# Four layers of linear and memory attention: where VectorE's weight maxima, idle TensorE time, cleared keys and the reading product are put

## The chip, the cores and the metric

The kernel runs on one core of one Trainium2 chip. The metric is the device time of one execution in microseconds (us); a time given without more is the median of several runs. The engines are called TensorE (PE in the profile, its weight loads PEld), VectorE (DVE), ScalarE (ACT), GpSimd (POOL) and SyncE (SP, which here only issues DMAs). On chip a tensor lies in SBUF or, as the output of TensorE, in one of eight PSUM banks.

## The reference

The input has 2048 rows of 640 columns: 32 heads of 20. Layers A, B, A, B follow each other, each added to its input:

```python
x = x + A(layernorm(x)); x = x + B(layernorm(x))     # twice, with the same weights

def A(x, wqkv, wo):                                  # linear attention
    q, k, v = split(x @ wqkv)                        # per head
    phi = lambda t: where(t > 0, t + 1, exp(t)) + 1e-6
    kv, z = einsum("hsd,hse->hde", phi(k), v), sum_s(phi(k))
    return ((phi(q) @ kv) / (phi(q) @ z + 1e-6)) @ wo

def B(x, wq, wk, wv, wo, beta):                      # 4 segments of 512 rows
    for each segment:
        a_dot = softmax(q k^T / sqrt(20) + causal) v
        a_mem = (phi(q) M) / (phi(q) z + 1e-6)       # memory of the segments before
        o = sigmoid(beta) a_mem + (1 - sigmoid(beta)) a_dot
        M, z = M + phi(k)^T v, z + sum(phi(k))
    return o @ wo
```

## The kernel before

**Streams and queues.** Two Python generators, one for the dense work and one for attention, are stepped in turn by their planned costs; a generator may be woven with an auxiliary one, which is advanced `per` steps after each step of the main one. A `pause(n)` is n empty steps. So the order in which instructions are *traced* is written by hand, and on TensorE that order is the order of its queue (`MANUAL = ("PE",)`). The queues of the other engines are put in order at compile time by a list scheduler with a model of durations: an instruction that is ready early in that model may stand ahead of others that were traced before it. `issue_after(ins)` keeps the instructions of a block that run on the engine of `ins` behind `ins`. Each queue is worked off in order.

**Precision.** Most products are made of three f16 products: each f32 operand is split in an upper f16 half (written by ScalarE) and a lower one (written by VectorE). Weights are scaled by a power of two first, and for that `w_prep` (L228 to L274) loads a weight into a `stage` buffer (two of them), takes five maxima over 640 columns on VectorE (L240) and one over these (L245), turns it on TensorE (L249), takes the maximum of the row (L251), spreads it with a product of one column (L255), makes scale and inverse (L258 to L261), and writes the ten halves (L266, L267). The pauses between these steps are `wait` auxiliary steps.

**The opening (`opening`, L1108 to L1192)** is layer A's first half on the input: four segments of four row tiles. A row tile is normed (`moments`, `normed`), turned by five identity products (`turn`, L321) and split. The key weights A k come first. `g_first` makes per segment the keys (`keys`: two halves of 320 columns, 15 products each at L397; `phi_a` on ScalarE and VectorE, L409 to L412; the lower half at L534, which is kept as `self.keyed`), the queries (`queries`, stored to DRAM as `pqd`), and adds to the memory the products of keys and normed input (`memory`, ten groups of 12 products, L571; taken up by VectorE at L591 or L593). The other weights are prepared as auxiliary steps: A q in segment 0, A v and A o in segment 1, B v and B q in 2, B k, B o and the gates (`gates`, L196 to L212) in 3. There the auxiliary generator goes two steps for one.

**The merge (`merge`)** ends the last segment: the sum of keys is spread over all rows (L636) and inverted (L638), the memory is scaled and split (`ge`, L652 to L655), multiplied by the value weights (L669), masked to the heads (L677) and written as two f16 halves into a row tile `kt` with zeros around (L674 to L681), and multiplied by the output weights (L702, L708; split into `wm` at L711, L712).

**Reading (`p_read`, L729 to L743)**: a row tile of stored queries is loaded (`p_load`, L726), multiplied by the spread key sum `zb` (L735), summed per head (L738), inverted (L739, L740) and multiplied by the inverse (L741). Then `a_second` turns it, multiplies it by `wm` (L397), adds the residual, and norms it for layer B. `a_head` reads the first three row tiles of a segment, `a_second` the fourth. In segment 0 the three are loaded by `a_head`, in the later ones within `p_read`.

**Layer B** projects a segment (`b_project`) while attention runs on the one before: the row maxima (L966, and L972 on VectorE), their split (L981, L982) and turn (L990), the scores and their exponentials (L1007, L1011), the causal selection on GpSimd (L1018) and the weighted sum (L1034). All row-shaped buffers share one pool of 11 (`ROWS`).

Of the kernel before, what the change touches and what calls it, by code (L numbers as in the profile page):

```python
# [10 lines left out]
F16 = mybir.dt.float16  # L11
# [116 lines left out]
def pause(n):  # L128
    for _ in range(n):
        yield 0.0  # L130
# [12 lines left out]
class Kernel:  # L143
# [84 lines left out]
    def w_prep(self, key, stage, w, wait=0, behind=None):  # L228
# [23 lines left out]
        yield 100.0  # L252
        yield from pause(wait)
        pb = self.bank()
# [56 lines left out]

    def turn(self, src, dst, i):
# [302 lines left out]
    def merge(self, L, wv, wo, memory, fill):  # L617
# [24 lines left out]
        for n in range(2):  # L642
# [4 lines left out]
            for c in range(C):  # L647
# [7 lines left out]
                nc.vector.tensor_tensor(t[:, c, 1, :HN], e, t[:, c, 0, :HN], op=OP.subtract)  # L655
        L["zb"] = zb
        for _ in memory:
            pass
        yield from filled(1)
        kt = []  # L660
        for t in range(C):
            p = self.bank()
            lo, hi = LO[t] * DH, (HI[t] + 1) * DH
            first = True
            for n in range(2):
                a, b = max(lo, n * HN), min(hi, (n + 1) * HN)
                for c in range(C if a < b else 0):
                    for k, m in ((0, 0), (0, 1), (1, 0)):
# [3 lines left out]
                        first = False  # L672
            k2 = sb.tile([P, 2, SEG], F16, tag="row", name="kt", bufs=ROWS)
            nc.vector.memset(k2, 0.0)  # L674
            e = sb.tile([P, 512], F32, tag="er", name="ke", bufs=3)[:, :hi - lo]
# [5 lines left out]
            L["split"] = nc.vector.tensor_tensor(k2[:, 1, P:P + hi - lo], e, k2[:, 0, P:P + hi - lo], op=OP.subtract)  # L681
            kt.append(k2)
            yield 15 * (hi - lo) * COL
# [45 lines left out]
    def p_read(self, L, s, i, o, pq=None):  # L729

        nc = self.nc
        if pq is None:
            pq = self.p_load(L, s, i)
        with self.tc.issue_after(L["split"].ins):
            nc.gpsimd.tensor_tensor(pq, pq, L["zb"][:, :D], op=OP.mult)  # L735
        q3 = pq.rearrange("p (h e) -> p h e", e=DH)
        rc = self.sb.tile([P, H], F32, tag="rca", name="rca", bufs=3)
        nc.vector.tensor_reduce(rc, q3, axis=AX.X, op=OP.add)  # L738
        nc.vector.tensor_scalar(rc, rc, 1e-6, 1 / P_ONE, op0=OP.add, op1=OP.mult)  # L739
        nc.vector.reciprocal(rc, rc)  # L740
        nc.gpsimd.tensor_tensor(q3, q3, rc[:, :, None].to_broadcast([P, H, DH]), op=OP.mult)  # L741
        o.append(pq)
        yield 0.0  # L743


    def a_head(self, L, s, box):

        while L["zb"] is None:
            yield 0.0
        box.update(o=[], oT=[])  # L750
        pq = [None] * 3
        if L["kt"] is None:
            pq = [self.p_load(L, s, i) for i in range(3)]
        while L["kt"] is None:
            yield 0.0
        box["oT"].append(self.new_oT())
        for i in range(3):
# [350 lines left out]
    def opening(self, src, stage, L, box):  # L1108
# [3 lines left out]
        def prep(key, keep=True):  # L1112
            w = self.w_tile(key) if keep else stage.tile([P, C, 2, D], F16, tag="split", name="split", bufs=1)
            if keep:
                self.w[key] = w
            yield from self.w_prep(key, stage, w, 0 if key[0] == "A" and keep else 6 if key == ("B", "o") else 3,
                                   {("A", "q"): self.lower, ("A", "v"): self.keyed}.get(key))

# [19 lines left out]

        self.lower = self.keyed = None
        cur = [None, self.x_t(), self.xs_t(0)]  # L1140
# [5 lines left out]
        x += [self.load_x(src, 0, i) for i in range(1, NT)]  # L1146
        first = self.normed(*m)
        yield from self.turn(first, cur[1], 0)
        with self.tc.high_priority():
            for _ in range(4):  # L1150
                next(k)
            with self.tc.issue_after(self.last.ins):
                m = self.moments(x[1])
            with self.tc.issue_after(self.taken.ins):
                w("k")
# [20 lines left out]
        for s in range(NSEG):  # L1176
            nxt = []
            if s == 0:
                q = a("q")
                n = self.norms(src, 1, nxt, 6)  # L1180
                aux = chain(o, islice(q, 3), pause(8), islice(q, 1), pause(2), islice(n, 1), pause(4), q, n)
            elif s == 1:
                aux = chain(self.norms(src, 2, nxt, 6), a("v"), a("o"), late())
            elif s == 2:
# [147 lines left out]
```

## Time and profile before

| | |
|---|---|
| median of 3 runs | 1723.12 us (1722.1 to 1726.43) |
| the profiled execution | 1722.49 us, span 1720.7 us |
| mean granted TensorE clock | 0.995 |
| TensorE busy | 1643.5 us (96%) |
| VectorE busy | 1244.5 us (72%) |
| ScalarE busy | 993.7 us (58%) |
| GpSimd busy | 535.6 us (31%) |
| HBM read, written | 109.32 MB, 78.64 MB |

How to read the lines that follow. A line of a timeline gives the start from the span's begin, the duration, engine, source line, operation, output<-inputs, and how many were merged into it; in square brackets, how long the engine sat idle before and what released it. A line of stretches gives the window, its length, and per engine the busy time with the number of instructions in brackets, in the order PE, PEld, DVE, ACT, POOL, then the granted clock of TensorE, the share of the DMA engines' time and GB/s. A line of waits gives who waited for whom, the sum in us, how often, and the longest. A line of groups gives the sum and the mean in ns of one, then the idle time before them and its causes. "SPq" is the time in which SyncE issues a DMA, not the transfer.

### The profile page before, as it was taken

How to read it: one execution, taken by the hardware profiler on the slowest of the kernel's cores; microseconds unless marked ns; L12 is line 12 of the kernel's file. 1: busy time of each engine (PE TensorE's matmuls, PEld its weight loads, DVE VectorE, ACT ScalarE, POOL GpSimd, SP SyncE). 2: the span in 40 equal slices, each digit the busy share in tenths (PEclk: the TensorE clock that was granted, in tenths of full speed). 3: DMA queues.
4: the chain of work that ended last, by engine and by line, in shares of the span. 5: the costliest groups of instructions: out<-in, count | busy, mean ns of one | idle time of the engine just before them, and what ended most of it. 6: DMA issues, size and time to landing. Idle time of an engine off the chain costs nothing.

```text
span 1720.7 us, 36268 instructions
## 1 busy us (share of the span) xinstructions
PE 1643.5 (96%) x13032; PEld 1031.4 (60%) x13032; DVE 1244.5 (72%) x3951; ACT 993.7 (58%) x1888; POOL 535.6 (31%) x1050
## 2 busy tenths in 40 slices
PE   6989989999999999999999999999999999999998
PEld 4767756554465566556556777766446545645555
DVE  7788886397787678759874466837787777878773
ACT  5666533346656646667775554433675575666673
POOL 3432224032223332334352311221431432233452
PEclk9999999999999999999999999999999999999999
DMA  6424654422222331453211303523132323223432
GB/s 216 154 86 151 225 205 142 138 93 73 95 78 69 109 121 55 126 178 97 75 52 44 110 31 123 196 92 124 64 106 77 112 82 109 93 84 111 145 104 93
DMA packets 110365, 190.89 MB, mean 111 GB/s; under 512 B 14172, under 2 KB 69596, under 8 KB 107624
## 3 DMA queue, kind: packets, MB, share of 16 engines
q1 hardware_dynamic: 97704, 142.68, 25.6%
q0 software_dynamic: 3264, 24.91, 4.0%
q10 hardware_dynamic: 9216, 20.98, 3.1%
q8 instruction: 103, 1.69, 0.4%
q14 instruction: 78, 0.64, 0.1%
HBM read 109.32 MB, written 78.64 MB: 109 GB/s over the span
## 4 chain that ended last, share of the span: by engine, by line
PE 71%; DVE 14%; ACT 7%; issue 3%; DMA 3%; POOL 2%; SPq 0%; ACTq 0%; POOLq 0%; DVEq 0%
PE ps L397 29%; PE ps L383 13%; PE ps L1034 7%; PE ps L571 5%; PE ps L1007 4%; PE ps L966 3%; PE ps L321 3%; ACT pe L1011 3%; DVE ps L972 2%; PE ps L448 2%; PE ps L851 2%; PE ps L1047 1%; DVE wmx L240 1%; DVE e L412 1%; DVE split L267 1%
## 5 line engine op out<-in xcount | busy, mean ns | idle before, releaser
L972 DVE CUSTOM_DVE_ANT_0 ps<-ps,maskw 128x384 f32<-128x384 f32 (+3 forms) x1024 | 473.1, 519 | 39.3 <-PE ps L966 36.6
L1011 ACT ACTIVATE pe<-ps,lsc 128x512 f32<-128x512 f32 x640 | 395.8, 697 | 76.2 <-PE ps L1007 74.8
L397 PEld LDWEIGHTS <-xT 128*128 128x128 f16 x2880 | 281.5, 98 | 115.5 <-issue 6.3
L1018 POOL TENSOR_SCALAR_AFFINE_SELECT pe<-pe 128x256 f32<-128x256 f32 (+1 forms) x640 | 229.6, 366 | 369.4 <-ACT pe L1011 362.8
L397 PEld LDWEIGHTS <-oT 128*128 128x128 f16 x1920 | 185.6, 98 | 82.1 <-issue 5.9
L1034 PE MATMUL ps<-pe,v 128*32 128x512 f32 (+3 forms) x2048 | 164.3, 436 | 12.5 <-POOL pe L1018 7.3
L397 PE MATMUL ps<-w_Ak,xT 128*128 128x320 f16 x960 | 142.8, 306 | 3.2 <-ACT w_Ak L266 1.2
L972 DVE DVE_READ_ACCUMULATOR2_ANT mg<- 128x1 f32 x1024 | 144.4, 141 | 0.0
L397 PE MATMUL ps<-wm,oT 128*128 128x320 f16 x960 | 141.0, 300 | 3.2 <-DVE oT L326 2.3
L397 PE MATMUL ps<-w_Bo,oT 128*128 128x320 f16 x960 | 142.4, 301 | 1.8 <-ACT oT L325 1.1
L383 PE MATMUL ps<-xT,w_Bq 128*128 128x512 f16 x600 | 140.3, 380 | 2.8 <-ACT r L421 1.6
L397 PE MATMUL ps<-w_Bv,xT 128*128 128x320 f16 x960 | 139.7, 300 | 1.2 <-DVE otok L1054 1.2
L571 PE MATMUL ps<-pk,xs 128*128 128x321 f16 (+1 forms) x960 | 139.4, 303 | 0.9 <-DVE pk L534 0.5
L383 PE MATMUL ps<-xT,w_Bk 128*128 128x512 f16 x600 | 138.4, 380 | 1.2 <-ACT pe L1011 1.2
L397 PE MATMUL ps<-w_Aq,xT 128*128 128x320 f16 x960 | 137.9, 300 | 0.1
L966 PE MATMUL ps<-ks,qs 60*128 60x512 f16 (+3 forms) x1024 | 123.2, 298 | 6.7 <-ACT pe L1011 3.2
L571 PEld LDWEIGHTS <-xs 128*128 128x128 f16 x960 | 93.7, 98 | 39.6 <-issue 2.1
L816 DVE SCALAR_TENSOR_TENSOR nat<-ps,nat 128x512 f16<-128x512 f32 x80 | 55.1, 689 | 82.6 <-ACT nat L815 82.4
L1034 PEld LDWEIGHTS ps<-pe,v 128*32 128x32 f32 x2048 | 65.4, 109 | 74.4 <-issue 39.3
L412 DVE SCALAR_TENSOR_TENSOR e<-e,r 128x320 f32<-128x320 f32 x128 | 68.2, 533 | 56.5 <-ACT r L411 56.2
L1007 PE MATMUL ps<-qs,ks 62*128 62x512 f16 (+3 forms) x1024 | 106.5, 300 | 2.2 <-ACT pe L1011 1.1
L815 ACT ACTIVATE nat<-ps 128x512 f16<-128x512 f32 x80 | 48.3, 603 | 88.5 <-PE ps L383 72.3
(197 smaller groups left out, 2395.9 us busy)
## 6 DMA issues: line engine op xcount, KB each, us to landing
x<-xn ACTq DMA_DIRECT2D x48, 320.0 KB
qs<-qd SPq DMA_DIRECT2D x128, 120.0 KB
ks<-kd SPq DMA_DIRECT2D x128, 120.0 KB
xo<-x SPq DMA_DIRECT2D x48, 320.0 KB
pqi<-pqd SPq DMA_DIRECT2D x32, 320.0 KB
qd<-nat SPq DMA_DIRECT2D x40, 256.0 KB
kd<-nat SPq DMA_DIRECT2D x40, 256.0 KB
x<-in_A_x SPq DMA_DIRECT2D x16, 320.0 KB
```

Of the source, the lines that this page charges most:

```text
L321: nc.tensor.transpose(pt[:, (c - c0) * P:(c - c0 + 1) * P], src[:, c * P:(c + 1) * P], self.ident)
L383: nc.tensor.matmul(p, w[:, c, a, t * P:(t + 1) * P], xT[:, c, b, :], start=k == 0, stop=k == 3 * C - 1)
L397: nc.tensor.matmul(p, xT[:, c, a, i * P:(i + 1) * P], w[:, c, b, n * HN:(n + 1) * HN], start=k == 0, stop=k == 3 * C - 1)
L412: nc.vector.scalar_tensor_tensor(e, e, 1.0, r, op0=OP.min, op1=OP.add)
L571: nc.tensor.matmul(p, xs[:, i, a, c * P:(c + 1) * P], pk[i][:, b, cols], start=i == 0 and a == b, stop=i == NT - 1 and a == 1)
L816: nc.vector.scalar_tensor_tensor(nat[:, 1], p, QK_SHIFT, nat[:, 0], op0=OP.mult, op1=OP.subtract)
L966: nc.tensor.matmul(bs[par][:, a:a + n], qs[r, p, i * P:(i + 1) * P], ks[r, p, :n], start=True, stop=True)
L972: nc.vector.tensor_tensor_reduce(bs[par][:, a:a + n], bs[par][:, a:a + n], self.maskw[:, SEG - n:], 1.0, NEG, OP.add, OP.max, G["mg"][:, p ...
L1007: nc.tensor.matmul(b[:, a:a + n], ks[r, p, j * P:(j + 1) * P], qs[r, p, j * P:], start=True, stop=True)
L1011: nc.scalar.activation(e, b, AF.Exp, scale=self.lsc)
L1018: nc.gpsimd.affine_select(d, d, pattern=pat, compare_op=OP.is_ge, fill=0.0, base=0, channel_multiplier=-1)
L1034: nc.tensor.matmul(G["pv"][32 * h4:32 * h4 + 32, j * P:], v[j][:, h * E1:h * E1 + 32], G.pop((p, par, j)), start=j == 0, stop=j == 2, skip ...
```

## The change

- `w_prep`: for the output weight of B the pause between the maximum's turn and its spreading is 12 auxiliary steps instead of 6.
- `opening`: the five maxima of A v are kept behind the last key step of segment 0 (`self.first`) instead of the one that was traced last when the preparation begins, in segment 1.
- `busy(n)`: n products of the f32 identity with itself (128x128) into a bank that nobody reads; 10 before the first turn, 5 after it, 3 behind the preparation of the key weights' scale.
- `merge`: the five `kt` tiles are taken together ahead of the products, and GpSimd clears the two stretches of each that are read as zeros and not written, where VectorE cleared the whole tile.
- `merge`, `a_head`: the three loads of segment 0 are traced in the merge, ahead of the remaining memory products (`L["pre"]`).
- `p_read`: the product with `zb` stays on GpSimd for these three tiles and goes to VectorE for the 13 others of each of the two layers A. There the bound of `issue_after` (behind the last `kt` half) holds, since both are on VectorE.

```diff
 w_prep
-        yield from pause(wait)
+        yield from pause(2 * wait if key == ("B", "o") else wait)
         pb = self.bank()
         nc.tensor.matmul(pb[:, :1], self.ones, m2, start=True, stop=True)
...
+    def busy(self, n):
+        p = self.bank()
+        for _ in range(n):
+            self.nc.tensor.matmul(p[:, :P], self.ident, self.ident, start=True, stop=True)
...
 merge
         L["zb"] = zb
+        L["pre"] = [self.p_load(L, 0, i) for i in range(3)]
         for _ in memory:
             pass
         yield from filled(1)
-        kt = []
-        for t in range(C):
+        kt = [sb.tile([P, 2, SEG], F16, tag="row", name="kt", bufs=ROWS) for _ in range(C)]
+        for t, k2 in enumerate(kt):
+            nc.gpsimd.memset(k2[:, :, 64:P], 0.0)
+            nc.gpsimd.memset(k2[:, :, P + (HI[t] + 1 - LO[t]) * DH:320], 0.0)
+        for t, k2 in enumerate(kt):
             p = self.bank()
...
-            k2 = sb.tile([P, 2, SEG], F16, tag="row", name="kt", bufs=ROWS)
-            nc.vector.memset(k2, 0.0)
...
-            kt.append(k2)
...
 p_read
+        eng = nc.gpsimd
         if pq is None:
-            pq = self.p_load(L, s, i)
+            pq, eng = self.p_load(L, s, i), nc.vector
         with self.tc.issue_after(L["split"].ins):
-            nc.gpsimd.tensor_tensor(pq, pq, L["zb"][:, :D], op=OP.mult)
+            eng.tensor_tensor(pq, pq, L["zb"][:, :D], op=OP.mult)
...
 a_head
-        while L["zb"] is None:
-            yield 0.0
         box.update(o=[], oT=[])
-        pq = [None] * 3
-        if L["kt"] is None:
-            pq = [self.p_load(L, s, i) for i in range(3)]
         while L["kt"] is None:
             yield 0.0
+        pq = L["pre"] if s == 0 else [None] * 3
...
 opening
-                                   {("A", "q"): self.lower, ("A", "v"): self.keyed}.get(key))
+                                   {("A", "q"): self.lower, ("A", "v"): self.first}.get(key))
...
-        self.lower = self.keyed = None
+        self.lower = self.keyed = self.first = None
...
         first = self.normed(*m)
+        self.busy(10)
         yield from self.turn(first, cur[1], 0)
+        self.busy(5)
         with self.tc.high_priority():
             for _ in range(4):
                 next(k)
+            self.busy(3)
...
             elif s == 1:
+                self.first = self.keyed
                 aux = chain(self.norms(src, 2, nxt, 6), a("v"), a("o"), late())
```

## The prediction

> **What bounds the kernel now.** I read the page's busy shares first (its first line), then the stretches of ten microseconds, then TensorE's waits, and last the timelines of the places that the change touches.
>
> ```profile
> PE 1643.5 (96%) x13032; PEld 1031.4 (60%) x13032; DVE 1244.5 (72%) x3951; ACT 993.7 (58%) x1888; POOL 535.6 (31%) x1050
> ```
> ```profile
> 100.00:110.00 10.00, 5.30 (x35) 3.48 (x34) 9.46 (x15) 7.89 (x16) 6.76 (x9) 0.80 0.00 1
> 220.00:230.00 10.00, 5.08 (x38) 3.41 (x35) 5.00 (x10) 0.21 (x1) 1.66 (x2) 0.95 0.63 234
> 230.00:240.00 10.00, 8.68 (x48) 5.71 (x49) 10.00 (x25) 5.66 (x10) 3.52 (x3) 0.71 0.01 2
> 240.00:250.00 10.00, 9.16 (x104) 7.26 (x102) 9.80 (x22) 3.42 (x8) 0.92 (x3) 1.00 0.51 183
> ```
> ```profile
> PE ps L1034 <- POOL pe L1018: 7.3, 12, 1.2
> PE ps L255 <- DVE wm L251: 6.6, 2, 6.2
> PE ps L249 <- DVE wm L245: 6.5, 2, 4.7
> ...
> PE pm L990 <- DVE m L982: 2.9, 2, 1.5
> ```
>
> TensorE is busy for 96% of a span of 1720.7 us, so 77 us of idle time are all that any wait removed can return (span less 1643.5), and its order is written by hand: a microsecond saved at one place arrives at the end unless a later wait takes it. Two waits stand out: 4.7 us on a transpose of weight maxima (L249) and 6.2 us on the broadcast of one (L255). The stretches show where: 100 to 110 and 220 to 240, and there the granted clock falls to 0.80 and 0.71, so each wait is also paid in slow products behind it.
>
> **The opening (identity products).**
>
> ```profile
> 7.83 1.33 PE L321 MATMUL ps<-ident,xh 128*128 128x128 f32 x5 [7.83 <-ACT xh L370]
> ...
> 15.67 6.14 PE L397 MATMUL ps<-w_Ak,xT 128*128 128x320 f16 x26 [0.17 <-DVE w_Ak L267]
> ...
> 58.78 16.46 PE L397 MATMUL ps<-w_Aq,xT 128*128 128x320 f16 x120
> ```
> ```profile
> 2.73 0.23 DVE L167 CAST ident<-ident 128x128 f16<-128x128 f32 x1 [1.38 <-DMA ident<-in_const]
> ...
> 15.08 4.24 DVE L267 SCALAR_TENSOR_TENSOR w_Ak<-stage,scl_Ak,w_Ak 128x320 f16<-128x320 f32 x9
> ```
> ```profile
> 12.86 4.63 ACT L266 ACTIVATE w_Ak<-stage,scl_Ak 128x320 f16<-128x320 f32 x10 [3.28 <-DMA stage<-in_A_wqkv]
> 18.80 0.53 ACT L409 ACTIVATE e<-ps,inv_Ak 128x320 f32<-128x320 f32 x1 [1.31 <-PE ps L397]
> ...
> 21.85 0.53 ACT L409 ACTIVATE e<-ps,inv_Ak 128x320 f32<-128x320 f32 x1 [0.67 <-PE ps L397]
> ```
>
> The first 26 projection products take 6.14 us, 0.236 each; later the same form takes 16.46/120 = 0.137. So they run largely at the slow rate, although the stretch's clock column does not say so. The identity is there at 2.73 and the first turn starts at 7.83: 5.1 us in which ten products fit. A product of two f32 operands of this size is not in the trace; a transpose of the same size takes 1.33/5 = 0.27 slow. It is bounded by that 0.27 and by its double, 0.54; I take the middle, 0.40, since only one row bears on it. Ten then end at 6.7, before the turn; at 0.54 they end at 8.1 and delay it by 0.3. The five and the three others lie under the round trip of the maxima and add 0.5 at worst, as the upper bound has it. If the array is warm at 13.5, the products are held by VectorE's lower halves (end 19.32) rather than by the array: the first half can end at 17.5, when ScalarE's ten copies end (12.86 + 4.63), not 18.80, and the second near 19.9 (19.3 and the queue on ScalarE), not 21.85. ScalarE and VectorE carry the chain from there to 43 us, so I take **-1.9** (bounds -2.3 and +0.8).
>
> **The maxima of the values' weights (`self.first`).**
>
> ```profile
> 27.07 2.94 SPq L236 DMA_DIRECT2D stage<-in_A_wqkv  x5
> ```
> ```profile
> 42.34 0.72 DVE L534 SCALAR_TENSOR_TENSOR pk<-e,k_scl,pk 128x320 f16<-128x320 f32 x1 [0.64 <-ACT pk L547]
> ```
> ```profile
> L240 DVE TENSOR_REDUCE wmx<-stage 128x1 f32<-128x640 f32 x40 | 31.4, 807 | 1.7 <-DMA stage<-in_B_wk 1.0 <-DMA stage<-in_B_wo 0.7
> ```
> ```profile
> 108.61 0.37 PE L249 MATMUL ps<-ident,wm 128*1 128x128 f32 x1 [4.70 <-DVE wm L245]
> 108.78 4.21 PE L397 MATMUL ps<-w_Ak,xT 128*128 128x320 f16 x15
> ...
> 117.31 11.65 PE L571 MATMUL ps<-pk,xs 128*128 128x321 f16 x84
> ```
>
> The five reductions (5 x 0.807 = 4.0 us) are bound behind a key step of segment 1 and so stand in a VectorE queue that is 9.46 of 10 busy, while TensorE waits 4.70. Bound behind the last key step of segment 0 (42.34) they may go as soon as their data, issued at 27.07, is there: far earlier. In front of them stands segment 0's key step, behind them the residuals of the query weights; those feed the 120 products at 58.78, whose 16.46 us cover the rest, so I cost the move at nothing (4.0 if all five fell ahead of the query weights). The gain: 4.70 of wait, and 4.21 - 15 x 0.137 = 2.15 of slow clock, 6.85 in all. What is late next is the last pair of keys on VectorE, which has 4.0 us less to do and the other weight's five reductions (L240 again) still between. The products at 117.31 could start at 110.5; I let 0.85 of it be lost, one reduction's length: **-6.0** (bounds -6.9 and -2.9).
>
> **The output weight's pause, and the merged keys.**
>
> ```profile
> 231.32 0.58 PE L255 MATMUL ps<-wm,ones 1*128 1x1 f32 x2 [6.24 <-DVE wm L251]
> ...
> 249.88 2.45 PE L669 MATMUL ps<-xT,w_Av 128*128 128x80 f16 x35 [0.65 <-DVE xT L655]
> ...
> 264.98 1.94 PE L397 MATMUL ps<-wm,oT 128*128 128x320 f16 x13 [1.57 <-DVE oT L326]
> ```
> ```profile
> 225.29 0.17 DVE L211 TENSOR_SCALAR cg<-cg 128x8 f32<-128x8 f32 x1 [4.96 <-ACT cg L209]
> ...
> 231.05 0.22 DVE L251 TENSOR_REDUCE wm<-ps 1x1 f32<-1x128 f32 x1
> ```
> ```profile
> L674 DVE MEMSET kt<- 128x512 uint32 x10 | 4.8, 485 | 0.5
> L194 POOL MEMSET v<- 128x32 f32 x16 | 2.1, 167 | 21.9 <-DVE ge L652 21.9
> ```
> ```profile
> 1101.67 1.94 PE L397 MATMUL ps<-wm,oT 128*128 128x320 f16 x13 [0.71 <-DVE oT L326]
> ```
>
> Two auxiliary steps follow each step of segment 3, so six more pauses put L255 behind three more memory products, 3 x 12 x 0.137 = 4.9 us. The wait of 6.24 shrinks to about 1.3, and with it goes the slow clock (some 2 us, as above). But the cause, VectorE standing 4.96 us behind L211, is not touched, and after it VectorE is full (10.00, then 9.80 of 10). TensorE reaches the merge 7 us earlier and waits there for L655, which moves only by what VectorE no longer does ahead of it: one clearing of 0.485 and the last of the output weight's residuals. Of the 8 us I count **-1.5**. Bounds: -5.0, if VectorE uses the time, and +0.5, if the new wait is long enough for the clock to fall.
>
> The row of 4.70 idle was followed by slow products, the row of 1.57 was not: 13 in 1.94 us is 0.149 each. The Trainium skill, "TensorE: Matmul & The Clock Gate", Part 1, puts the bound at an idle window of about 3.4 us. By that rule the new wait at the merge, which I put at 3 to 5 us, would cost up to another 2 us, and this part would come out at +0.5 instead of -1.5.
>
> The five clearings are 5 x 0.485 = 2.4 us of VectorE in each merge, in a queue that TensorE waits for (0.65 and 1.57). GpSimd does them in ten short ones; L194 clears 32 f32 columns in 0.167, so 1.7 us at most on an engine that is 0.92 of 10 busy there; each needs a free row buffer first, and the weight loads of attention queue behind it, on an engine nearly idle. The first merge returns **-2.0** (bounds -2.4 and 0), the second **-0.7**, all of its one wait (0 at the other end). The three early loads stay on SP's queue, traced a few products sooner, and their readers come after the merge: nothing.
>
> **The product in reading.**
>
> ```profile
> L735 POOL TENSOR_TENSOR pqi<-pqi,zb 128x640 f32<-128x640 f32 x32 | 49.1, 1546 | 82.4 <-ACT pkt L845 30.6 <-issue 29.5 <-DMA pqi<-pqd 13.9
> L738 DVE TENSOR_REDUCE rca<-pqi 128x32 f32<-128x640 f32 x32 | 25.5, 804 | 8.2 <-POOL pqi L735 8.2
> L555 DVE TENSOR_TENSOR z<-z,e 128x320 f32<-128x320 f32 x30 | 15.6, 520 | 0.7
> ```
> ```profile
> 375.86 1.55 POOL L735 TENSOR_TENSOR pqi<-pqi,zb 128x640 f32<-128x640 f32 x1
> ```
> ```profile
> 375.90 1.54 DVE L981 TENSOR_SCALAR m<-mg 128x16 f16<-128x16 f32 x1
> ```
> ```profile
> 26.66 1.40 POOL L479 TENSOR_TENSOR xs<-xh,xs 128x640 f16<-128x640 f32 x1 [0.81 <-ACT xs L478]
> ```
> ```profile
> 22.83 0.49 DVE L412 SCALAR_TENSOR_TENSOR e<-e,r 128x320 f32<-128x320 f32 x1 [0.63 <-ACT r L411]
> ...
> 27.45 0.96 DVE L412 SCALAR_TENSOR_TENSOR e<-e,r 128x320 f32<-128x320 f32 x1 [0.93 <-ACT r L411]
> ```
> ```profile
> 615.06 1.54 POOL L735 TENSOR_TENSOR pqi<-pqi,zb 128x640 f32<-128x640 f32 x1 [1.64 <-DMA pqi<-pqd]
> ```
>
> Of 32 products, the three early ones of each layer stay on GpSimd; 26 move. Each frees 1.546 us of GpSimd and costs VectorE between 0.804 (a reduction over the same 640 columns) and 2 x 0.520 = 1.04 (this operation on half the columns, twice); I take 0.85, nearer the full-width row: 22 us of VectorE in all, 16 of the 26 beside attention. Against it: VectorE's waits for the product (8.2) go, and so do collisions such as L981 at 375.90, which lasted exactly as long as the GpSimd product beside it; TensorE then waited up to 1.5 for L982, or up to 1.2 for a selection queued behind the product (7.3 and 2.9 in all). Half of these 10.2 us, 5, could go. The new wait: VectorE, in order, now waits for the load (1.64 at 615.06), and the row maxima of attention queue behind it. I take 3 of cost against 5: **-2.0** (bounds -6 and +5).
>
> **Sum**, against the profiled execution's own 1722.49 us (the median of the runs is 1723.12): -1.9 - 6.0 - 1.5 - 2.7 - 2.0 = -14.1, so **1708.4**. The best bounds together give -23.3, or 1699.2; the worst +3.4, or 1725.9. About 5 us (0.3%) is what a measurement of this kernel can tell from no change.
>
> **Rivals.** (1) VectorE becomes the bound in reading: its 22 us reach TensorE whole, and two waits per layer like the 1.64 come on top (6.6), with no relief. Then -12.1 + 28.6 = +16.5, 1739.0. It decides from the point where VectorE has no slack beside attention; for it speak the hand-ordered row maxima, against it the 28% of the span that VectorE idles and the collisions that end. Chance 0.08. (2) The queue of VectorE takes the time back: the merge gives nothing, reading nothing, and the maxima only 3: -1.9 - 3 = -4.9, 1717.6. For it: VectorE at 9.46 and 10.00 in both stretches. Chance 0.16. (3) The maxima stay where they are, because the program that orders VectorE's queue keeps them behind more urgent work: the term of -6.0 falls away, 1714.4. For it: nothing but that the order is not written in the kernel; chance 0.07. (4) The 4.96 behind L211 goes as well, because the gates are traced later now: another -4, 1704.4. For it: it is the root of the second stall; against it: its own release is unchanged. Chance 0.15. (5) The two engines collide over the moved product: L412, an instruction with two operands, takes 0.49 alone and 0.96 at 27.45, beside GpSimd's L479. If each of the 16 products beside attention is lengthened by that 0.47, 7.5 us are added: -14.1 + 7.5 = -6.6, 1715.9. Chance 0.06. The Trainium skill, "SBUF — State Buffer", section "Who interferes with whom", states such a rule, against this edit: a VectorE instruction with two SBUF inputs contends with a GpSimd instruction that reads SBUF, and the second to issue waits; the doubled L412 agrees. The forecast has 0.48.
>
> **How the numbers follow.** Faster is the forecast, (3), (4), (5) and half of (2), whose value lies on the limit: 0.84; no change, the other half, 0.08; slower, (1), 0.08. The range 1700 to 1720 holds the forecast and (2) to (5), and leaves out (1) and the sums near the bounds.
>
> **What would show it.** Right: PE's wait on L249 near 108 gone and the clock column at 1.00 there; five L240 between 43 and 62; the first 26 products in about 4 us; L255's wait under 2 us, with a new wait on L655; no L674 on VectorE; L735 on VectorE near 0.85. Wrong: L735 on VectorE with long idle time before it (rival 1), L240 still at 101 to 107 (rival 3), or a new wait before 60 us behind the moved maxima.

## The result and the profile after

The changed kernel takes 1712.07 us (median of 4 runs, 1712.04 to 1712.97) beside 1723.91 us before (4 runs, 1722.1 to 1726.43): a ratio of 0.9932 with a 95% interval of 0.9914 to 0.9949, so 11.8 us faster. The forecast was 1708.4 in a range of 1700 to 1720. The profiled executions are 1712.08 us (span 1710.4, granted clock 0.995) after and 1722.49 before, 10.4 apart. The total came near; the terms did not, as the rest shows.

In the changed file most lines stand a little lower: the turn L321 is now L326 and its VectorE copy L331, the projections L397 are L402, the memory L571 is L576, `ge` and its halves L652 to L655 are L657 to L660, the merged keys L669 are L678, the product of reading L735 is L742, the row maxima's split L981 and L982 are L984 and L985, its turn L990 is L993, the causal selection L1018 is L1021, the weighted sum L1034 is L1037, the products for the row maxima L966 are L969, the turn of layer B's keys L843 is L846, the second product of reading L741 is L748. L240 to L274 kept their numbers; the identity products are L317.

The page's first line, six stretches of ten microseconds, and some of TensorE's waits, all of the changed kernel:

```profile
PE 1647.0 (96%) x13068; PEld 1037.8 (61%) x13068; DVE 1257.2 (74%) x3967; ACT 992.9 (58%) x1888; POOL 503.2 (29%) x1044
```
```profile
100.00:110.00 10.00, 8.48 (x64) 6.00 (x62) 5.72 (x10) 8.67 (x17) 7.59 (x10) 1.00 0.06 21
140.00:150.00 10.00, 6.95 (x52) 5.16 (x51) 10.00 (x21) 6.65 (x16) 4.54 (x8) 1.00 0.98 347
220.00:230.00 10.00, 8.96 (x66) 6.25 (x65) 7.68 (x13) 0.21 (x1) 4.10 (x3) 1.00 0.33 128
230.00:240.00 10.00, 8.97 (x94) 6.89 (x92) 10.00 (x27) 4.93 (x10) 1.57 (x7) 1.00 0.01 2
240.00:250.00 10.00, 4.63 (x40) 4.05 (x40) 9.86 (x25) 5.52 (x14) 1.46 (x4) 0.67 0.48 136
570.00:580.00 10.00, 8.99 (x51) 4.19 (x48) 5.84 (x24) 6.12 (x12) 4.42 (x10) 0.83 0.36 123
```
```profile
PE ps L678 <- DVE xT L660: 4.0, 5, 1.0
PE ps L255 <- DVE wm L251: 3.3, 3, 1.5
...
PE ps L402 <- DVE xT L331: 3.0, 3, 1.8
PE ps L1037 <- POOL pe L1021: 2.9, 8, 0.6
...
PE ps L678 <- ACT xT L659: 2.4, 2, 1.6
...
PE ps L846 <- DVE pkT L427: 2.1, 3, 1.3
...
PE pm L993 <- DVE m L985: 0.3, 1, 0.3
```

The stretch 100 to 110 is healed (8.48 busy, clock 1.00), and so are 220 to 230 (8.96 busy for 5.08) and 230 to 240 (clock 1.00 for 0.71). Three are worse: 140 to 150, where TensorE was 10.00 busy before and is 6.95 now; 240 to 250, where the merge now waits on VectorE's copies (L678 on L660) at clock 0.67; and 570 to 580, where the clock was 1.00 before. The wait for masked rows fell from 7.3 to 2.9, and that of the turn L993 on the split of the row maxima from 2.9 to 0.3.

The same TensorE instruction, looked up in both timelines, shows how the lead grows and shrinks (start in us):

| instruction | before | changed | lead |
|---|---|---|---|
| first memory products, segment 0 (the last five of the group) | 41.08 | 39.78 | 1.3 |
| first memory products, segment 1 | 117.31 | 110.65 | 6.7 |
| first memory products, segment 3 | 215.51 | 212.83 | 2.7 |
| first product with `kt`, first merge | 252.16 | 250.25 | 1.9 |
| second group of products with `wm` after that merge | 266.98 | 263.17 | 3.8 |
| memory update of layer B, first pass | 492.30 | 485.46 | 6.8 |
| the same, one segment on | 649.95 | 645.50 | 4.5 |
| the same, second pass | 1184.02 | 1178.88 | 5.1 |
| weighted sum after the second reading | 1490.62 | 1481.23 | 9.4 |
| last turn | 1698.68 | 1688.35 | 10.3 |

Most of the lead of A v's maxima is given back by 215 us. The merge takes another 0.8 up to its first product with `kt` and returns 1.9 behind it, where VectorE no longer clears; the two readings bring most of the rest. These are leads of single executions: a second profile of the changed kernel reaches the memory products of segment 1 at 111.96, 1.3 later than the first, and ends 0.7 sooner.

From 492 to 650 a lead of 2.3 is lost again, 1.7 of it at nine products of one group, here in the kernel before and in the changed one:

```profile
581.06 2.12 PE L383 MATMUL ps<-xT,w_Bk 128*128 128x512 f16 x9
```
```profile
574.25 3.80 PE L388 MATMUL ps<-xT,w_Bk 128*128 128x512 f16 x9
```

The same two short waits (0.42 and 0.56) stand shortly ahead of these products in both kernels, and in the second profile of the changed kernel, behind the same waits, the nine take 2.12 again. So this loss belongs to the execution and not to the change.

### The profile page after: what moved, and what is told of

The parts are those of the page before. It is cut to its first block, busy times and chain, and to the rows that moved or that the text cites. A ratio compares the mean times of both kernels' runs of the same rounds, so it can differ in the third digit from the quotient of the medians.

```text
span 1710.4 us, 36361 instructions
## 1 busy us (share of the span) xinstructions
PE 1647.0 (96%) x13068; PEld 1037.8 (61%) x13068; DVE 1257.2 (74%) x3967; ACT 992.9 (58%) x1888; POOL 503.2 (29%) x1044
## 4 chain that ended last, share of the span: by engine, by line
PE 68%; DVE 14%; ACT 9%; issue 3%; DMA 3%; POOL 2%; SPq 1%; ACTq 0%; POOLq 0%; DVEq 0%
PE ps L402 26%; PE ps L388 13%; PE ps L1037 7%; PE ps L576 4%; PE ps L1010 4%; PE ps L969 3%; PE ps L326 3%; ACT pe L1014 3%; DVE ps L975 2%; PE ps L453 2%; PE ps L854 2%; PE ps L1050 1%; DVE e L417 1%; DVE split L267 1%; DVE wmx L240 1%
## 5 line engine op out<-in xcount | busy, mean ns | idle before, releaser
L402 PEld LDWEIGHTS <-xT 128*128 128x128 f16 x2880 | 280.9, 98 | 116.4 <-issue 10.0
L1021 POOL TENSOR_SCALAR_AFFINE_SELECT pe<-pe 128x256 f32<-128x256 f32 (+1 forms) x640 | 232.3, 371 | 368.4 <-ACT pe L1014 359.4
L402 PEld LDWEIGHTS <-oT 128*128 128x128 f16 x1920 | 185.4, 98 | 78.8 <-issue 6.5
L1037 PE MATMUL ps<-pe,v 128*32 128x512 f32 (+3 forms) x2048 | 163.2, 436 | 7.9 <-POOL pe L1021 2.9
L402 PE MATMUL ps<-w_Ak,xT 128*128 128x320 f16 x960 | 139.2, 301 | 4.0 <-DVE w_Ak L267 1.3
L402 PE MATMUL ps<-w_Bo,oT 128*128 128x320 f16 x960 | 140.8, 299 | 1.4 <-ACT oT L330 0.7
L402 PE MATMUL ps<-wm,oT 128*128 128x320 f16 x960 | 140.9, 299 | 1.3 <-DVE mg L975 0.3
L402 PE MATMUL ps<-w_Bv,xT 128*128 128x320 f16 x960 | 141.2, 301 | 0.1
L402 PE MATMUL ps<-w_Aq,xT 128*128 128x320 f16 x960 | 137.8, 299 | 2.4 <-DVE xT L331 1.8
L576 PE MATMUL ps<-pk,xs 128*128 128x321 f16 (+1 forms) x960 | 137.7, 300 | 1.1 <-DVE pk L539 0.7
L969 PE MATMUL ps<-ks,qs 60*128 60x512 f16 (+3 forms) x1024 | 122.5, 297 | 7.2 <-ACT pe L1014 3.2
L576 PEld LDWEIGHTS <-xs 128*128 128x128 f16 x960 | 92.8, 97 | 38.9 <-issue 2.0
L1037 PEld LDWEIGHTS ps<-pe,v 128*32 128x32 f32 x2048 | 66.1, 109 | 67.7 <-issue 38.4
L388 PEld LDWEIGHTS <-w_Bk 128*128 128x128 f16 x600 | 57.4, 98 | 67.2 <-issue 7.7
```

The lines of the kernel that those rows point to most:

```text
L388: nc.tensor.matmul(p, w[:, c, a, t * P:(t + 1) * P], xT[:, c, b, :], start=k == 0, stop=k == 3 * C - 1)
L402: nc.tensor.matmul(p, xT[:, c, a, i * P:(i + 1) * P], w[:, c, b, n * HN:(n + 1) * HN], start=k == 0, stop=k == 3 * C - 1)
L576: nc.tensor.matmul(p, xs[:, i, a, c * P:(c + 1) * P], pk[i][:, b, cols], start=i == 0 and a == b, stop=i == NT - 1 and a == 1)
L969: nc.tensor.matmul(bs[par][:, a:a + n], qs[r, p, i * P:(i + 1) * P], ks[r, p, :n], start=True, stop=True)
L1021: nc.gpsimd.affine_select(d, d, pattern=pat, compare_op=OP.is_ge, fill=0.0, base=0, channel_multiplier=-1)
L1037: nc.tensor.matmul(G["pv"][32 * h4:32 * h4 + 32, j * P:], v[j][:, h * E1:h * E1 + 32], G.pop((p, par, j)), start=j == 0, stop=j == 2, skip ...
```

## The experiments

Each of the first five undoes one part of the change, so a time above 1712 is what that part is worth; the early loads of segment 0 were not undone by themselves. The changed kernel was also run again (the last of this section): its nine runs together have a median of 1712.04 and spread from 1710.34 to 1713.02, so differences below about 1 us between kernels tell nothing. The kernel before was taken again with each group of runs, with medians of 1722.61 to 1725.35; the ratios refer to these.

**Without the identity products**

```diff
-        self.busy(10)
...
-        self.busy(5)
...
-            self.busy(3)
```

> The changed kernel without its 18 identity products (busy(10), busy(5), busy(3) left out); the output is the same. From the two traces the memory products of segment 0 start 1.29 us earlier after the change, and 0.3 to 0.45 of that is there already in the weight maxima, before any product of w_Ak. Theory (the products bring TensorE in warm, worth what the trace shows): 0.8 to 1.0 us slower than the 1712.07 of the changed kernel, about 1713.0, with the first 26 products of w_Ak back near 6.1 us. Rival (the products only bring the clock's fall forward, since the stretch 10 to 20 us shows 0.83 after the change and 1.00 before): no change or up to 0.5 faster, 1711.6 to 1712.1, with the clock of that stretch back at 1.00. My forecast had priced them at 1.9: 1714.0.

Measured: 1711.25 (1710.43 to 1712.19), ratio to the kernel before 0.9929 [0.9917, 0.9942]. The products are worth nothing that these runs can tell. TensorE's timeline and two stretches of two microseconds, first of the changed kernel, then without the products:

```profile
15.21 5.07 PE L402 MATMUL ps<-w_Ak,xT 128*128 128x320 f16 x26 [0.55 <-DVE w_Ak L267]
```
```profile
14.00:16.00 2.00, 1.35 (x7) 0.72 (x7) 1.55 (x5) 2.00 (x5) 0.54 (x3) 0.66 0.45 155
16.00:18.00 2.00, 2.00 (x9) 1.18 (x8) 2.00 (x6) 1.04 (x3) 0.00 (x0) 0.50 0.00 0
```
```profile
15.74 4.58 PE L402 MATMUL ps<-w_Ak,xT 128*128 128x320 f16 x26 [0.17 <-DVE w_Ak L267]
```
```profile
14.00:16.00 2.00, 1.21 (x5) 0.54 (x5) 1.55 (x5) 2.00 (x5) 0.88 (x3) 1.00 0.66 236
16.00:18.00 2.00, 2.00 (x11) 1.19 (x10) 2.00 (x6) 1.56 (x4) 0.00 (x0) 1.00 0.00 0
```

In this pair the 26 begin 0.5 earlier with the products and take 0.5 longer: the clock stood at 0.50 up to 18 us, after five microseconds of small pieces with gaps. Both rows end at 20.3. The 1.00 of the second pair of stretches doesn't mean that TensorE ran at full rate there: without the products the column reads 1.00 from the start, while the first five turns take 1.33 and the next five 0.74. And the 6.14 of the kernel before was not the price of a cold start as such: four profiles without identity products show 6.14, 5.31, 4.58 and 5.82 for these 26, the ten with them 4.67 to 5.50.

**A v's maxima released in their own segment**

```diff
-                                   {("A", "q"): self.lower, ("A", "v"): self.first}.get(key))
+                                   {("A", "q"): self.lower, ("A", "v"): self.keyed}.get(key))
...
-                self.first = self.keyed
```

> The changed kernel with A v's five maxima again released by the key of their own segment (self.keyed in place of self.first); all else stays changed. Theory A (the trace: 5.4 us are gained up to 117 us and most of it is given back between 140 and 150, because VectorE there waits for the load of the constants and for B v's weight): the undone part costs only what reached segment 3, 1.4 to 2.7 us, about 1714; the PE wait for xT at 146 (1.82) is gone, the wait of L249 of 4.7 is back. Theory B (my forecast's term: the whole gain arrives): 5 to 6 us slower, about 1718.

Measured: 1714.05 (1713.95 to 1714.71), 0.9947 [0.9934, 0.9959]. Theory A: the part is worth 2.0, not 6. Its timeline has the old wait again, and its stretch 140 to 150 is full:

```profile
107.83 0.37 PE L249 MATMUL ps<-ident,wm 128*1 128x128 f32 x1 [5.37 <-DVE wm L245]
108.00 4.20 PE L402 MATMUL ps<-w_Ak,xT 128*128 128x320 f16 x15
```
```profile
140.00:150.00 10.00, 10.00 (x79) 7.72 (x78) 10.00 (x21) 6.71 (x16) 3.58 (x7) 1.00 0.91 320
```

**B o's pause at its old length**

```diff
-        yield from pause(2 * wait if key == ("B", "o") else wait)
+        yield from pause(wait)
```

> The changed kernel with the short pause of before for B o (wait, not 2 * wait). Theory A (the wait of 6.24 at L255 comes back, but the waits of L678 on xT of 4 to 6 us and the stretch at clock 0.67 go): 0.5 to 2 us slower, about 1713.5. Theory B (the pause only moves the stall and puts the product loop at the low clock): 0 to 2 us faster, about 1711. In both, no PE wait of over 0.7 us on xT between the memory's last products and the keys of A v.

Measured: 1710.97 (1709.35 to 1712.13), 0.9928 [0.9915, 0.9941]: no difference that these runs can tell. The long pause turns one wait into many and no more. With the short one, the first merge of this run reads:

```profile
229.11 0.58 PE L255 MATMUL ps<-wm,ones 1*128 1x1 f32 x2 [6.30 <-DVE wm L251]
229.62 10.33 PE L576 MATMUL ps<-pk,xs 128*128 128x320 f16 x60
...
247.91 2.28 PE L678 MATMUL ps<-xT,w_Av 128*128 128x80 f16 x32 [0.89 <-DVE xT L660]
```

and in the changed kernel:

```profile
228.35 0.38 PE L255 MATMUL ps<-wm,ones 1*128 1x1 f32 x2 [1.04 <-DVE wm L251]
...
241.16 0.20 PE L678 MATMUL ps<-xT,w_Av 128*128 128x80 f16 x1 [1.64 <-ACT xT L659]
242.35 0.23 PE L678 MATMUL ps<-xT,w_Av 128*128 128x80 f16 x2 [1.00 <-DVE xT L660]
...
246.74 3.67 PE L678 MATMUL ps<-xT,w_Av 128*128 128x80 f16 x32 [1.04 <-DVE xT L660]
```

The last 32 products end at 250.2 and at 250.4: 5.3 us less of waiting at L255, paid back by six waits on the halves and by 32 products that take 3.67 for 2.28. The 0.89 with the short pause is above the 0.7 that was expected there.

**The merged keys cleared by VectorE**

```diff
-            nc.gpsimd.memset(k2[:, :, 64:P], 0.0)
-            nc.gpsimd.memset(k2[:, :, P + (HI[t] + 1 - LO[t]) * DH:320], 0.0)
...
+            nc.vector.memset(k2, 0.0)
```

> The changed kernel with the merged keys cleared whole by VectorE inside the loop, as before, five times in each of the two merges. Theory A (forecast: the clears stand on VectorE between the products and their scaling, about 0.98 us each, in the first merge near 2.0, in the second 0.7): 2.0 to 2.7 us slower, about 1714.5, with the wait of 1.57 on oT at the end of the first merge and 0.71 at the second back. Theory B (in the first merge the late w_Bo scaling now sets the end, so the clears fall in its shadow): 0.7 to 1.0 slower, all in the second merge, about 1713.

Measured: 1714.45 (1712.59 to 1715.28), 0.9946 [0.9932, 0.9961]: 2.4 slower, near the 2.7 of the forecast. The waits are the ones it named, 1.57 in the first merge and the rest in the second, as TensorE's waits of this run sum them (L679 is the clearing, among its groups; one takes 0.485, not the 0.98 of the expectation):

```profile
PE ps L402 <- DVE oT L331: 2.3, 2, 1.6
```
```profile
L679 DVE MEMSET kt<- 128x512 uint32 x10 | 4.8, 485 | 0.6
```

**The reading product on GpSimd**

```diff
-            pq, eng = self.p_load(L, s, i), nc.vector
+            pq, eng = self.p_load(L, s, i), nc.gpsimd
```

> The changed kernel with p_read's product of the rows that it loads itself back on GpSimd (eng stays nc.gpsimd). Theory A (the traces: from 275 to 650 us the lead grows by 0.7 and by up to 3 before a clock dip, from 1184 to 1420 it grows by 4.3): 3.5 to 5 us slower, about 1716.5, with the waits 1.47 and 1.48 of the product after the row maxima and 1.17 and 1.16 for the masked rows back. Theory B (my forecast's term of 2.0): about 1714. Theory C (GpSimd and VectorE only change places): within 0.7 of 1712.1.

Measured: 1723.4 (11 runs, 1719.06 to 1724.58), 0.9991 [0.998, 1.0002]: without this edit the other four together bring next to nothing in the median. Five of its runs, at a granted clock of 0.995 to 0.996, lie at 1719.06 to 1721.33; six, at 0.993 to 0.994, at 1723.4 to 1724.58. Against the changed kernel (0.994 to 0.995 in all runs) the edit is thus worth 7 to 9 us at a like clock, and 11 to 12.5 by the six runs at the lower one, more than any of the three theories had; why more than half of the runs have the lower clock is open. So the parts don't add up exactly: undone one by one, they cost 11.3, 2.4 and 2.0 by the medians, 15.7 together, where all bring 11.8. In the profiled executions this run (1719.06) lies 3.4 below the kernel before and 7.0 above the changed one. The waits of this run, which are those of the kernel before (7.3 and 2.9), and the place of one, VectorE's and GpSimd's timelines at 373 us:

```profile
PE ps L1037 <- POOL pe L1021: 7.3, 12, 1.2
...
PE pm L993 <- DVE m L985: 2.9, 2, 1.5
```
```profile
373.69 1.54 DVE L984 TENSOR_SCALAR m<-mg 128x16 f16<-128x16 f32 x1
```
```profile
373.63 1.57 POOL L742 TENSOR_TENSOR pqi<-pqi,zb 128x640 f32<-128x640 f32 x1
375.13 1.15 POOL L1021 TENSOR_SCALAR_AFFINE_SELECT pe<-pe 128x256 f32<-128x256 f32 x3
```

A VectorE instruction on 16 columns starts just after the GpSimd product and ends with it; three selections that TensorE wants stand behind the product. In the changed kernel the same step (VectorE, then the groups of the moved product and of the six that stayed):

```profile
372.13 0.17 DVE L984 TENSOR_SCALAR m<-mg 128x16 f16<-128x16 f32 x1
...
372.29 0.82 DVE L742 TENSOR_TENSOR pqi<-pqi,zb 128x640 f32<-128x640 f32 x1
```
```profile
L742 DVE TENSOR_TENSOR pqi<-pqi,zb 128x640 f32<-128x640 f32 x26 | 23.2, 897 | 1.0 <-DMA pqi<-pqd 1.0
...
L742 POOL TENSOR_TENSOR pqi<-pqi,zb 128x640 f32<-128x640 f32 x6 | 9.3, 1578 | 17.2 <-DMA pqi<-pqd 9.5 <-DVE zb L642 7.7
```

0.17 for 1.54, and VectorE waits for the loads 1.0 us in all. Of the 64 instructions of L984, four last more than 0.5 us in the run with GpSimd (1.54, 1.35, 1.54 and 1.36), all beside the product L742; in the changed kernel three do (0.63, 0.63 and 1.20), all beside GpSimd's second product, L748.

**The kernel before with the reading product on VectorE alone**

```diff
+        eng = nc.gpsimd
         if pq is None:
-            pq = self.p_load(L, s, i)
+            pq, eng = self.p_load(L, s, i), nc.vector
...
-            nc.gpsimd.tensor_tensor(pq, pq, L["zb"][:, :D], op=OP.mult)
+            eng.tensor_tensor(pq, pq, L["zb"][:, :D], op=OP.mult)
```

> The kernel before with the reading's product on VectorE as its only edit (rows that p_read loads itself; the first three rows stay on GpSimd as before). Theory A (this edit carries most of the gain, as undoing it cost 7.0 at the same granted clock and 11.3 in the median): 7 to 11 us faster than before, 1712 to 1716, waits of 1.47 and 1.48 at L990 and of 1.17 and 1.16 on the masked rows gone. Theory B (undoing it hurt only beside the other edits; alone it is worth my forecast's 2): about 1721.

Measured: 1714.85 (1713.37 to 1717.65) beside 1725.02, 0.9951 [0.9933, 0.9969]. Theory A, from the other side, and the waits fall as in the changed kernel (masked rows to 2.9, the turn of the row maxima to 0.3): this one edit carries 8 (by the ratio) to 10 us (by the medians) of the 11.8.

**The gates' constants in segment 2**

```diff
-            with self.tc.issue_after(self.keyed.ins):
-                self.gates()
...
+        def beta():
+            with self.tc.issue_after(self.keyed.ins):
+                self.gates()
+            yield 0.0
...
-                aux = chain(self.norms(src, 3, nxt, 6), prep(("B", "v"), False), prep(("B", "q"), False))
+                aux = chain(beta(), self.norms(src, 3, nxt, 6), prep(("B", "v"), False), prep(("B", "q"), False))
```

> The changed kernel with the gates' constants (cg, gate) loaded and raised in segment 2 and not behind the last key of segment 3, so VectorE no longer stands 5.15 us before L211. Theory A (VectorE's queue sets the end of the first merge: the copies of xT come late because of that stand): the waits of L678 on xT (4.0 and 2.4 in sum) shrink to under 2, the clock 0.67 of the stretch 240 to 250 us goes, 3 to 6 us faster, about 1707.5. Theory B (the chain from the memory's last products over 1/z, or w_Bo's scaling, sets it): within 0.7 of 1712.1.

Measured: 1706.01 (1704.32 to 1707.8), 0.9893 [0.9879, 0.9907]: 6.0 faster than the changed kernel. What the edit takes away is VectorE's stand ahead of L211, here in the changed kernel:

```profile
222.32 0.17 DVE L211 TENSOR_SCALAR cg<-cg 128x8 f32<-128x8 f32 x1 [5.15 <-ACT cg L209]
```

With the gates early L211 runs at 147 us without idle time, TensorE is 10.00 busy from 220 to 230, and the last 32 products, as slow as in the changed kernel, begin 6 us sooner than the 246.74 above:

```profile
240.77 3.79 PE L678 MATMUL ps<-xT,w_Av 128*128 128x80 f16 x32 [1.14 <-DVE xT L660]
```

Not all of these 6 us come from that stand. The spread of the key sum (L641), ahead of it, begins at 214.14 for 216.12, so 2.0 were there already, most of them gained between 110 and 167 us; 4.0 arise behind it. The waits of L678 on L660 stayed at 3.5, above the 2 that was expected, and the clock of 240 to 250 at 0.68.

**The late constants in a buffer of their own**

```diff
-    def setup_late(self, stage):
+    def setup_load(self, stage):
...
-        t = stage.tile([P, P + MW], F32, tag="stage", name="cst", bufs=2)
-        nc.sync.dma_start(t, self.const[:, P:])
+        self.cst = stage.tile([P, P + MW], F32, tag="cst", name="cst", bufs=1)
+        self.nc.sync.dma_start(self.cst, self.const[:, P:])
...
+                self.setup_load(stage)
```

> The changed kernel with the late constants (mask, blocks) in a buffer of their own, loaded in the opening, so that neither L184 (4.88 us idle on VectorE) nor B v's weight (2.92 idle) waits behind A v's written copy in the stage's two buffers. Theory A (these two waits are what gives the lead of A v's maxima back at 140 to 150): the PE waits of 1.82 and 0.86 on xT go, 2 to 3.5 us faster, about 1709.5. Theory B (VectorE's own work in that stretch, five scalings and ten maxima, gives it back): within 0.7 of 1712.1, with the same waits.

Measured: 1710.76 (1710.04 to 1711.2), 0.992 [0.9906, 0.9933]: 1.3 faster than the changed kernel, hardly more than its spread, so neither theory as it stood. VectorE's timeline shows why: two waits of the changed kernel (4.88 and 2.92) are replaced by one of 5.05, where B v's load, issued right behind the written copy of A v (at 123.32 and 122.94), is there 6.8 us later. First the changed kernel, then this one (where L240 is L243):

```profile
128.30 0.23 DVE L184 CAST maskw<-cst 128x128 bf16<-128x128 f32 x1 [4.88 <-DMA cst<-in_const]
...
132.96 0.82 DVE L240 TENSOR_REDUCE wmx<-stage 128x1 f32<-128x640 f32 x1 [2.92 <-DMA stage<-in_B_wv]
```
```profile
130.14 0.82 DVE L243 TENSOR_REDUCE wmx<-stage 128x1 f32<-128x640 f32 x1 [5.05 <-DMA stage<-in_B_wv]
```

VectorE's idle time there fell from 7.8 to 5.05, and TensorE's wait on xT at 146 from 1.82 to 0.41; the next rose from 0.86 to 1.44. So the loads that VectorE waits for set a part of the pace at 140 to 150; that a load ahead of A v's copy would return the rest was not tried. What was gained there is gone by the first merge: the memory products of segment 2 begin at 166.50 for 166.86, the first product with `kt` at 250.24 for 250.25.

**Both together**

The edit is the two diffs before this.

> Both of the two before (gates in segment 2, late constants in a buffer of their own) on the changed kernel. If both first theories hold and the stages are apart in time, the gains add: 5 to 9 us faster, about 1705. If VectorE's own work is the bound in both places: within 1 us of 1712.1.

Measured: 1702.76 (1702.24 to 1703.54), 0.9873 [0.9858, 0.9888]: 9.3 below the changed kernel, 22 below the kernel before beside it (1724.68), and the fastest of this study. It is 2 more than the two gains give (6.0 + 1.3); why is open.

**Both, with the short pause, and the same without identity products**

The edit is the two diffs before this with that of the pause, and then that of the identity products too.

> The kernel with gates in segment 2 and late constants in a buffer of their own (1702.76), and B o's pause at its old length. Theory A (the wait of 6.24 and 6.3 at L255 with the short pause was VectorE standing 5.15 before L211, which is gone; and the long pause is what puts w_Bo's scaling, four times 0.82, ahead of the last copies of xT): no wait of over 1 us at L255 nor at the products of w_Av, no stretch under 0.95 in the granted clock between 220 and 260 us, 3 to 6 us faster than 1702.76, about 1698.5. Theory B (the memory's evictions and the reciprocals hold VectorE there with or without L211): the wait at L255 stays at 3 us or more and the time is within 1.5 of 1702.8.

> The same without the 18 identity products. Theory A (they only move a clock window of half speed, as the first study of them showed, 0.8 below 1712.07 without them): within 1 us of the run with them, rather below, and the stretch 10 to 20 us at clock 1.00. Theory B (they bring 1 us or more once nothing later takes it back): 1 us or more slower.

Measured: 1705.17 (1704.58 to 1707.7), 0.9895 [0.9877, 0.9912], and 1704.55 (1703.22 to 1707.6), 0.9892 [0.9872, 0.9912]. With VectorE free, the wait at L255 (here L258) falls from 6.30 to 1.00 and the merge ends 0.5 sooner than with the long pause, as theory A has it; but the 3 to 6 us did not come, and the run is 2.4 slower, which neither theory had. In its profile the clock falls at 1640 to 1650 us (0.83), where 15 products take 3.80 for 2.20: 1.6 of the 1.8 by which the two profiled executions differ. What the other runs lost is open. The waits on the halves remain (0.63, 0.73, 0.89), so they are not made by the pause alone. The identity products again make no difference (0.6).

**The changed kernel again**

> The changed kernel itself once more, to see how far its runs spread, since the kernel without identity products (1711.25) and that with the short pause (1710.97) lie only 0.8 and 1.1 below it. If those two edits really cost time, 1712.0 to 1713.0 again; if they are worth nothing either way, runs between 1710 and 1713 with a median within 0.6 of 1711.

Measured: 1711.47 (1710.34 to 1713.02), 0.9925 [0.9912, 0.9939]: the second case. The two small differences above are within the spread.

## Why the prediction was right, and where its terms were not

The sum was -14.1; the profiled executions differ by 10.4, the medians by 11.8. Three terms were too large and one far too small; that they made up for each other, so that the total came near, was luck.

| term | forecast | shown |
|---|---|---|
| identity products | -1.9 | 0 (undone: 1711.25) |
| A v's maxima | -6.0 | -2.0 (undone: 1714.05) |
| B o's pause | -1.5 | 0 (undone: 1710.97) |
| clearing on GpSimd | -2.7 | -2.4 (undone: 1714.45) |
| product in reading | -2.0 | -7 to -11 (undone: 1719.06 to 1724.58; alone: 8 to 10 below before) |

**Identity products.** The step that failed is "if the array is warm at 13.5", which was taken to last for the 26 products. Ten products take 4.63 us (20 records), within the upper half of the bound, and in this profile the array was warm: the first product of `w_Ak` takes 0.30 at 13.01, and 0.42 at 13.47 in the kernel before. But it had only small pieces with gaps from 8 to 14 us, and in all ten profiles with these products the clock falls to 0.50 between 12 and 20 us. By the rows of two microseconds the spell lasts 3.4 us in seven of them (here 0.66, 0.50 and 0.99) and 6.8 in three. That the gaps cause it was not tested by itself. The Trainium skill, "TensorE: Matmul & The Clock Gate", Part 1, knows only these two states, full and half, where a single core is busy, and says that its window of about 3.4 us runs freely, so that the number of slow products differs from run to run; the spells of 3.4 and 6.8 us and the four values from 4.58 to 6.14 without the products agree.

**A v's maxima.** The move went as forecast: the five reductions run at 47.84 to 60.65, between 43 and 62, the wait at L249 is gone, the clock is 1.00. The sum stopped at the products that began at 117.31, where the trace has a lead of 5.4 from this stage (6.7 less the 1.3 of the opening). The failed step is that nothing was priced behind them: TensorE, 6 us earlier, meets VectorE's stretch at 139 to 156, which had moved by almost nothing, since VectorE now stands for two loads (7.8 us idle). In the kernel before it came to both later and found them there, the first one here without idle time:

```profile
131.16 0.22 DVE L184 CAST maskw<-cst 128x128 bf16<-128x128 f32 x1
```

The prediction had named a later wait as the condition ("unless a later wait takes it") and looked for it no further than those products. Rival (2), VectorE's queue taking the time back, is what happened here.

**The pause.** The new wait on the halves came, as forecast (3 to 5 us; it is 6.4 in seven pieces), and the clock fell behind it, which by the rule of the Trainium skill that the prediction cites was to make this part +0.5 and not -1.5. The rule was the better of the two: the part is worth nothing. Only no single wait of 3.4 us stood there: the longest was 1.64, with TensorE busy for 0.43 us between 239.5 and 243.3. Rival (4) was wrong: L211 waits 5.15 instead of 4.96. Its price was right: of the 6 us that the gates in segment 2 bring, 4.0 arise behind that stand.

**The clearing** was right in size (2.4 for 2.7, with a spread of 1) and in place.

**Reading.** The prices were right: 26 x 0.897 = 23.2 us on VectorE, 22 forecast. Two choices were not. Half of the 10.2 us of waits were to go; 7.0 went (7.3 to 2.9, 2.9 to 0.3). And 3 were charged for VectorE's wait on the loads; it waits 1.0, and what TensorE waits for more is 1.4 (L846 on VectorE 1.1 to 2.1, L969 on VectorE 1.7 to 2.1). So 5.6 net by these waits. In all, TensorE's idle time (span less busy) is 70.5 us in the profiled execution with GpSimd and 63.4 in the changed kernel: 7.1, the whole of the 7.0 by which the two differ. So the mis-sized step is the net of the waits, 2.0 forecast and 7 measured. That the medians differ by 11.3 goes with the lower clock of six of the runs, which the term had left out; its cause is not shown. The collision of rival (5) is real but goes mainly the other way. The Trainium skill, "SBUF — State Buffer", section "Who interferes with whom", says of a VectorE instruction in a two-port mode, which a `tensor_scalar` can enter, and GpSimd that the one that issues first keeps the shared ports for its whole instruction; L984 at 373.69 (1.54 beside GpSimd's 1.57, 0.17 in the changed kernel) agrees, though the profile doesn't show its mode. The edit removes the four such pairs with this product. What it adds is small: 26 x (0.897 - 0.82) = 2.0 us on VectorE. Rival (1), VectorE as the bound in reading, was wrong: with 23.2 us more of such products on VectorE, TensorE's idle time fell.

## What to carry to other kernels

When a wait is removed, follow the engine that caused it to its next rendezvous, and check whether its own loads are due by then: a lead that one engine gains is kept only as far as the others have slack; here most of it was gone after 30 us. A long instruction on GpSimd costs what stands behind it and beside it, not its own length; look for short instructions that last as long as a neighbour. And when moving a stall seems to help, look for what holds the engine at its root: moving the pause was worth nothing, while freeing VectorE from one wait of 5.15 was worth 6.0, 4 of it behind that wait.

## What the runs showed of the hardware

- Warming TensorE and then feeding it in pieces was no gain: with identity products at 2.7 to 12.6 us the granted clock fell to 0.50 between 12 and 20 us in all ten profiles, for 3.4 us in seven and 6.8 in three, and the time was the same (1712.04, 1711.25 without them).
- The clock column does not show a slow start: without these products it reads 1.00 from the first instruction, while five turns take 1.33 there and 0.71 to 0.74 later.
- Short waits can lower the clock without one long one: between 239.5 and 243.3 us TensorE was busy for 0.43, in waits of 1.64, 1.00 and 0.73; the next rows of two microseconds, from 242 to 250, read 0.83, 0.50, 0.50 and 0.50, and 32 products took 3.67 for 2.28.
- The same waits can cost clock in one execution and none in the next: behind waits of 0.42 and 0.56 nine products took 3.80 in one profile of the changed kernel and 2.12 in another. Such a spell costs about 1.7 us. How many an execution has differs: runs of one kernel at 0.995 to 0.996 and at 0.993 to 0.994 lie about 4 us apart (1719.06 to 1721.33, 1723.4 to 1724.58).
- The same product of two 128x640 operands takes 0.82 on VectorE alone, 1.54 on GpSimd.
